# A recurrent attention followed by a token and channel mixer on one core: batch 0 in token slots on 64-row tiles, u of batches 1 to 3 transposed by DMA, another order

## The chip, the cores and the metric

The kernel runs on one core of one Trainium2 chip. The metric is the device time of one execution in microseconds (us). The engines are PE (TensorE, matrix products), DVE (VectorE), ACT (ScalarE), POOL (GpSimd) and SP, which here only issues transfers. Each engine works its own queue in order. An instruction whose operand isn't ready holds up everything behind it on that engine. ACT also issues some transfers.

## The reference

```python
# q, k, v, alpha: 4 batches x 8 heads x 768 tokens x 48, fp32
state = zeros(B, H, 48, 48)
for t in range(768):
    state = alpha[:, :, t, :, None] * state + k_t (outer) v_t
    y[:, :, t] = q_t @ state
x = y as (4, 768, 384)                       # heads side by side
xt = x.transpose(0, 2, 1)                    # batch, channel, token
h = max(xt @ w_tok1, 0) @ w_tok2             # 768 -> 256 -> 768 over tokens
u = x + h.transpose(0, 2, 1)
out = u + max(u @ w_ch1, 0) @ w_ch2          # 384 -> 1536 -> 384 over channels
```

## The kernel before

The recurrence is worked in chunks of 256 tokens: three chunks for each of 4 batches, n = 0 to 11, n = 3b + k. A chunk is loaded with two neighbouring tokens on each of the 128 partitions; the two are its slots. A half is 128 tokens: 64 partitions with both slots. In a chunk the decay is made explicit by cumulative sums of ln alpha: `E` is the exponential of the sum, `IE` that of its negative. q is scaled by E and k by IE (`scaled`, line 642). Then come

- the transposes of the scaled k and q (names `trk`, `trq`, matmuls on line 654, copied out of PSUM as `evk`, `evq`; from chunk 6 on transfers that transpose, `dk`, `dq`, line 664, with a copy `pq`),
- `G`, the products of keys and queries of a half (16 small matmuls, through `mm`, line 593), times a triangular mask (`mask`, line 700),
- `K`, the product of keys and values that goes into the state, and the state itself (`s`: first multiply, line 747; `sa`: add, line 750; `sm`: multiply by the decay, line 753),
- `ia`, `ib` (queries times the state) and `y` (masked G times v), summed in one PSUM bank, and its copy `x` (line 684 on ACT, 685 on DVE).

Batch 0 (`WIDE`, chunks 0 to 2) takes the cumulative sum for each token (768 columns, `cumw`). The other chunks multiply the two alphas of a partition first (`P`, line 578) and correct one slot (`k0a`, `q0r`, lines 634 and 638). For y and K the kernel wants the 128 tokens of a half on 128 partitions, while the loads have them as 64 partitions times two slots. So half of v (`vs0`, `vs1`) and of the scaled k (`ka`, `kb`, `kc`) is copied between partition halves, 64 rows by 384, by `copy` (lines 684, 685), on all twelve chunks.

The mixer of a batch: `t1` (w_tok1, line 787), `ht` (relu), `t2` (w_tok2, line 792), `u` (add of x, line 796), u transposed (`ut`), `c1` (w_ch1, line 811; 12 column blocks by two halves, three matmuls each), `rt` (relu, line 782 on ACT, 784 on DVE), `c2` (w_ch2, line 816; 6 row blocks by four groups of three matmuls), `o` (line 820), `st` (store). For batches 0 and 1 (`UP`) u is transposed by TensorE (`up`, line 803, 18 matmuls, and three copies); for 2 and 3 by two transfers each (`ux`, line 668).

Loads are fp32, 384 KB each: alpha, k, q and v of 12 chunks (line 534) and 16 pieces of the weights (lines 550 to 557), into 19 shared buffers (`in`). Weight pieces are cast to bf16 once (`cw`).

The order of the work isn't left to a scheduler. `build` declares the operations, and three tables say the rest: ORDER lists all operations in one sequence with a letter for the engine (t PE, v DVE, s ACT, g POOL, y SP), and so fixes each engine's queue; BUFS gives each operand its buffer; GATES is empty. Waits follow from data and from buffers used again. `shared` (called by `copy` and the two-operand operations on DVE and POOL) makes such an operation wait for the last one of the other of these two engines, since they share a port. So DVE and POOL take turns there, in ORDER's sequence.

ORDER of before also holds fillers (`f1_`, `f3_`: one or three matmuls of 128x128 by 512 columns on a tile of zeros, `fill`), whose results nobody reads: 38 matmuls, all ahead of the first `c1` of batch 0.

Of the kernel before, what the change touches and what calls it, by code (L numbers as in the profile page):

```python
# [97 lines left out]
NX = 6  # L98
KFN = 0
LAST = (3, 0)  # L100
UP = (0, 1)
# [9 lines left out]
WIDE = (0, 1, 2)  # L111

# [3 lines left out]
def build(g):  # L116
# [8 lines left out]
    def filler(nm, bank):  # L125
        return [P.op(f"f{z}_{nm}", {"PE": pe([512] * z)["PE"], "NONE": (0.0, 0.0)}, -100, writes=[bank],
                     emit=lambda e, z=z: g.fill(bank, z)) for z in (1, 3)]

    def attention(n):
# [5 lines left out]
        def O(name, eng, i, **kw):  # L135
            return P.op(f"{name}{n}", eng, pr(i), **kw)

        def fill(nm, bank):
            return filler(f"{nm}{n}", bank) if n < NB else []

        at, kt, qt, vt = V("in"), V("in"), V("in"), V("in")
        ld = {}
        for v, nm in ((at, "at"), (kt, "kt"), (qt, "qt"), (vt, "vt")):
            ld[nm] = P.op(f"ld_{nm}{n}", {"SP": (420.0, 420.0), "ACT": (374.0, 374.0)}, -90000.0 + 10 * n, writes=[v],
                          emit=lambda e, v=v, nm=nm: g.load(e, nm, v, b, k, ld[nm]), dma=("i", IN_NS, 1500.0, 650.0))
        la, E, IE = V("la"), V("E"), V("IE")
        pkk, pkq, vb = V("pkk"), V("pkq"), V("vb")
        k_in, q_in = [ld["kt"]], [ld["qt"]]
        if n in WIDE:
            lnp = O("ln", act(800, True), 0, writes=[la], reads=[at], preds=[ld["at"]], emit=lambda e: g.lnw(la, at))  # L150
            cb = V("pair")
            cum = O("cumw", pe([384] * 4 + [4] * 8 + [16]), 2, writes=[cb, E, IE], reads=[la], preds=[lnp] + fill("cumw", cb),
                    emit=lambda e: g.cumw(cb, la))
            e1 = O("E", act(768), 4, writes=[E], reads=[cb], preds=[cum], emit=lambda e: g.exps(E, cb, 1.0))
            et = O("Et", act(16), 6, writes=[E], reads=[cb], preds=[cum], emit=lambda e: g.exptot(E, cb))
            e2 = O("IE", act(768), 3, writes=[IE], reads=[cb], preds=[cum], emit=lambda e: g.exps(IE, cb, -1.0))
        else:
# [8 lines left out]
            e1 = et = O("E", act(400), 4, writes=[E], reads=[cb], preds=[cum], emit=lambda e: g.expE(E, cb))  # L166
            e2 = O("IE", act(384), 4, writes=[IE], reads=[cb], preds=[cum], emit=lambda e: g.expIE(IE, cb))
# [5 lines left out]
        kk = O("kk", either(dve(768), pool_tt(768)), 5, writes=[pkk], reads=[kt, IE], port=True, preds=k_in + [e2],  # L173
               emit=lambda e: g.scaled(e, pkk, kt, IE, wide))
        qq = O("qq", either(dve(768), pool_tt(768)), 5, writes=[pkq], reads=[qt, E], port=True, preds=q_in + [e1],
               emit=lambda e: g.scaled(e, pkq, qt, E, wide))
# [3 lines left out]
        if n < NX:  # L180
            bk, bq = V("one"), V("one")
            trk = O("trk", pe([128] * 8), 8, writes=[bk], reads=[pkk], preds=[kk] + fill("trk", bk),
                    emit=lambda e: g.trw(bk, pkk))
            evk = O("evk", either(dve(1024, True), act(1024)), 9, writes=[tpk], reads=[bk], preds=[trk],
                    emit=lambda e: g.trwev(e, tpk, bk))
            trq = O("trq", pe([128] * 8), 8, writes=[bq], reads=[pkq], preds=[qq] + fill("trq", bq),
                    emit=lambda e: g.trw(bq, pkq))
            evq = O("evq", either(dve(1024 * 1.065), act(1024 * 1.34)), 9, writes=[tpq], reads=[bq], preds=[trq],
                    emit=lambda e: g.qev(e, tpq, g.bank(bq).bitcast(BF16)))
        else:  # L190
            evk = O("dk", {"SP": (1240.0, 1240.0)}, 9, writes=[tpk], reads=[pkk], preds=[kk],
                    emit=lambda e: g.xbar(tpk, pkk), dma=("x", 1400.0, 1180.0, 480.0))
            tqx = V("tpk")
            xq = O("dq", {"SP": (1240.0, 1240.0)}, 9, writes=[tqx], reads=[pkq], preds=[qq],
                   emit=lambda e: g.xbar(tqx, pkq), dma=("x", 1400.0, 1180.0, 480.0))
            evq = O("pq", either(dve(1024), act(1024 * 1.35, True), {"POOL": (1100.0, 1140.0)}), 9.5, port=True, writes=[tpq], reads=[tqx], preds=[xq],
                    emit=lambda e: g.qev(e, tpq, g.t(tqx)))
        gtm = V("gtm")
        masks = []
        for hf in range(2):  # L200
            gp = V("pair")
            G = O(f"G{hf}_", pe([128] * 4), 10 + hf, writes=[gp], reads=[tpk, tpq], preds=[evk, evq] + fill(f"G{hf}", gp),
                  emit=lambda e, hf=hf, gp=gp: g.gmm(gp, tpk, tpq, hf), mode="G")
            masks.append(O(f"mask{hf}_", dve(1024), 12 + hf, writes=[gtm], reads=[gp], preds=[G],
                           emit=lambda e, hf=hf, gp=gp: g.mask(gtm, gp, hf)))
        nst = 2 if k < NB - 1 else 1
        kp = V("pair")
# [4 lines left out]
        vsw = lambda hf, preds: shift(f"vs{hf}_", 10, [vb], [vt], preds, lambda e: g.vswap(e, vb, vt, hf))  # L212
        turned = n >= KFN
        if turned:
            vs = [vsw(hf, [vc]) for hf in range(2)]
            kx, kp_in = None, [kk, vc, vs[0]]
            if nst == 2:
                kx = V("kt")
                ka = shift("ka", 9, [kx], [pkk], [kk], lambda e: g.kturn(e, kx, pkk, 0))
# [137 lines left out]
    for b in range(B):  # L357
        mixer(b)
# [516 lines left out]
```

## Time and profile before

| | us |
|---|---|
| median of 3 runs | 167.82 |
| lowest and highest | 167.51, 168.41 |
| the profiled execution, first to last instruction (span) | 165.0 |

| engine | busy us | share of the span |
|---|---|---|
| PE | 156.2 | 95% |
| DVE | 121.2 | 73% |
| ACT | 96.2 | 58% |
| POOL | 68.7 | 42% |

The profile is of one execution. Its slices divide the span into 40 equal parts of 4.125 us; a digit is the busy share in tenths. In a row of the chain stand the start, the length and the engine with the line; in a row of the groups the line, engine, operation, operands, count, then busy us, the mean ns of one, and the idle time before with what ended it. In a row of a stretch stand its bounds, its length, and busy us with the count of instructions for each engine. A timeline row has start, length, engine, line, operation, operands, count. "SPq" is the transfer queue of SP.

### The profile page before, as it was taken

The numbers are of one execution on the slowest core, as the hardware profiler recorded it, in microseconds if no ns is written. First come the engines' busy times: TensorE is split into PE (matmuls) and PEld (weight loads), VectorE is DVE, ScalarE is ACT, GpSimd is POOL, SyncE is SP. The second block draws the span as 40 slices with busy tenths as digits, with TensorE's granted clock in tenths as the row PEclk, the third lists the DMA queues.
The fourth block names the chain that finished last, engine by engine and source line by source line (L and its number), as shares of the span: only waits on it lengthen the run. The fifth ranks groups of instructions, "written<-read, shape, count | busy, mean of one in ns | idle before, by whom it ended". The sixth has DMA issues, their size and how long they took to land.

```text
span 165.0 us, 4235 instructions
## 1 busy us (share of the span) xinstructions
PE 156.2 (95%) x1683; PEld 99.2 (60%) x1683; DVE 121.2 (73%) x210; ACT 96.2 (58%) x186; POOL 68.7 (42%) x84
## 2 busy tenths in 40 slices
PE   7969769999999999999999999999999999999992
PEld 2435446666666766576666666666666656656662
DVE  4098989989898898798878999989492455524422
ACT  3599987998877837939887746913614001514110
POOL 4025659497217475792388528973300000000000
PEclk9999999999999999999999999999999999999999
DMA  4999999999999999999989996898001136200213
GB/s 121 324 325 325 337 347 316 365 327 352 371 335 347 326 315 226 307 252 264 136 198 255 211 250 120 219 181 183 0 4 48 49 75 157 105 0 0 99 72 119
DMA packets 74531, 34.48 MB, mean 209 GB/s; under 512 B 67984, under 2 KB 73488, under 8 KB 74512
## 3 DMA queue, kind: packets, MB, share of 16 engines
q1 hardware_dynamic: 50576, 23.30, 55.2%
q10 hardware_dynamic: 23936, 10.91, 24.3%
q8 instruction: 13, 0.21, 0.5%
q14 instruction: 6, 0.05, 0.1%
HBM read 25.17 MB, written 4.72 MB: 181 GB/s over the span
## 4 chain that ended last, share of the span: by engine, by line
PE 83%; DMA 4%; SPq 3%; POOL 2%; issue 2%; ACT 2%; DVE 1%; POOLq 0%; DVEq 0%
PE ps L816 29%; PE ps L811 29%; PE ps L593 14%; PE ps L792 5%; DMA in<-in_v_dram 4%; PE ps L787 4%; SPq L534 3%; PE ps L654 1%; PE ps L803 1%; POOL pkk L642 1%; DVE gtm L700 1%; POOL vb L685 1%; ACT x L684 1%; POOL ss L753 1%; ACT E L626 0%
## 5 line engine op out<-in xcount | busy, mean ns | idle before, releaser
L816 PE MATMUL ps<-wc,rt 128*128 128x384 bf16 (+1 forms) x300 | 54.7, 320 | 0.0
L811 PE MATMUL ps<-ut,wc 128*128 128x384 bf16 x288 | 51.3, 326 | 0.0
L782 ACT ACTIVATE rt<-ps 128x384 bf16<-128x384 f32 x54 | 24.4, 490 | 35.4 <-PE ps L811 34.7
L811 PEld LDWEIGHTS <-wc 128*128 128x128 bf16 x288 | 27.1, 98 | 16.7
L816 PEld LDWEIGHTS <-rt 128*128 128x128 bf16 x300 | 27.5, 98 | 15.9
L700 DVE TENSOR_TENSOR gtm<-ps,mk 128x1024 bf16<-128x1024 f32 x24 | 28.7, 1219 | 4.8 <-PE ps L593 3.4
L784 DVE TENSOR_SCALAR rt<-ps 128x384 bf16<-128x384 f32 x42 | 21.7, 551 | 9.2 <-PE ps L811 9.2
L820 DVE TENSOR_TENSOR o<-ps,u 128x384 f32<-128x384 f32 (+1 forms) x25 | 13.1, 537 | 10.0 <-PE ps L816 9.1
L685 POOL CAST vb<-in 64x384 bf16<-64x384 f32 (+1 forms) x18 | 10.9, 608 | 15.2 <-DVE pkk L642 8.9
L593 PE MATMUL ps<-zs 128*128 128x512 bf16 x38 | 12.7, 452 | 2.9 <-DVE zs L496 1.1
L684 ACT CAST x<-ps 128x384 bf16<-128x384 f32 x17 | 7.8, 477 | 10.7 <-PE ps L593 10.5
L796 DVE TENSOR_TENSOR u<-ps,x 128x384 bf16<-128x384 f32 x24 | 11.8, 550 | 3.0 <-PE ps L792 3.0
L642 DVE TENSOR_TENSOR pkq<-in,E 128x768 bf16<-128x768 f32 x8 | 7.6, 954 | 5.4 <-ACT E L626 5.2
L787 PE MATMUL ps<-x,wt 128*128 128x384 bf16 x48 | 11.1, 325 | 0.5 <-DVE gtm L700 0.4
L684 ACT CAST vb<-in 64x384 bf16<-64x384 f32 (+1 forms) x18 | 11.1, 618 | 0.7 <-DMA in<-in_v_dram 0.2
L642 POOL TENSOR_TENSOR pkk<-in,IE 128x768 bf16<-128x768 f32 x5 | 9.1, 1816 | 4.9 <-DVE pkk L685 3.2
L753 POOL TENSOR_TENSOR ss<-tmp,E 128x384 bf16<-128x384 f32 x11 | 9.2, 833 | 3.2 <-DVE tmp L750 2.9
L750 DVE TENSOR_TENSOR tmp<-ps,ss 128x384 f32<-128x384 f32 x16 | 8.8, 552 | 1.0 <-PE ps L593 0.5
L792 PE MATMUL ps<-ht,wt 128*128 128x384 bf16 x48 | 9.5, 326 | 0.0
L593 PEld LDWEIGHTS <-gtm 128*128 128x128 bf16 x192 | 7.4, 96 | 2.7 <-DVE gtm L700 0.9
L593 PEld LDWEIGHTS <-tpk 48*64 48x64 bf16 x384 | 6.1, 106 | 4.9 <-issue 4.3
L593 PE MATMUL ps<-vb,gtm 128*128 128x48 bf16 x192 | 8.6, 183 | 0.4 <-DVE gtm L700 0.4
(91 smaller groups left out, 216.6 us busy)
## 6 DMA issues: line engine op xcount, KB each, us to landing
in<-in_moe_w_ch_dram SPq DMA_DIRECT2D x10, 384.0 KB, 6.2
in<-in_alpha_dram SPq DMA_DIRECT2D x9, 384.0 KB, 6.8
out_dram<-o SPq DMA_DIRECT2D x16, 192.0 KB, 2.5
in<-in_q_dram SPq DMA_DIRECT2D x7, 384.0 KB, 6.3
in<-in_v_dram ACTq DMA_DIRECT2D x7, 384.0 KB, 6.0
in<-in_k_dram ACTq DMA_DIRECT2D x6, 384.0 KB, 5.7
in<-in_k_dram SPq DMA_DIRECT2D x6, 384.0 KB, 6.2
in<-in_v_dram SPq DMA_DIRECT2D x5, 384.0 KB, 7.2
```

The source lines that it names most:

```text
L593: return self.pe.matmul(out, lhsT=lhsT, rhs=rhs, start=start, stop=stop, skip_group_check=True)
L642: self.shared(self.eng[e].tensor_tensor(self.t(dst)[:, :, :, 0:D], self.t(src).rearrange("p h s d -> p s h d"), bass.AP(tensor=f.tensor, o ...
L684: return self.act.copy(d, s)
L685: return self.shared(self.eng[e].tensor_copy(d, s))
L700: self.nc.vector.tensor_tensor(self.t(gtm)[:, hf, :, :], self.pair(gp).rearrange("p a (j t) -> p (a j) t", t=128), bass.AP(tensor=m.tensor ...
L782: self.act.activation(d, s, AF.Relu)
L784: self.nc.vector.tensor_scalar_max(d, s, 0.0)
L787: self.pe.matmul(self.bank(bank)[:, 0:HD], lhsT=self.wt1[:, kc, m * 128 : m * 128 + 128], rhs=self.t(x), start=(kc == 0), stop=(kc == NS - 1))
L792: self.pe.matmul(self.bank(bank)[:, 0:HD], lhsT=self.wt2[:, kc, i * 128 : i * 128 + 128], rhs=self.t(hts[kc]), start=(kc == 0), stop=(kc = ...
L811: self.pe.matmul(self.bank(bank)[:, 0:HD], lhsT=self.wc1[:, kc, mc * 128 : mc * 128 + 128], rhs=self.t(ut)[:, 3 * half : 3 * half + 3, kc, ...
L816: self.pe.matmul(self.bank(bank)[:, 0 : cz - ca], lhsT=self.t(rts[mc][0])[:, i * 128 : i * 128 + 128], rhs=self.wc2[:, mc, ca:cz], start=( ...
L820: self.nc.vector.tensor_tensor(self.t(o)[:, ca:cz], self.bank(bank)[:, 0 : cz - ca], self.t(u)[:, i % 3, ca:cz], ALU.add)
```

## The change

1. **Batch 0 by slot.** In chunks 0 to 2 G isn't formed for a half but for the keys of one slot: 64 keys of each half against the 128 queries of their own half, in the two halves of the partitions (`gslot`). The mask is shifted by one column for one of the slots (`maskslot`, a new table `mkw`). y is then the sum over both slots, with 64-row products: 32 matmuls of 48 columns for a chunk (`yslot`), and K 16 matmuls of 96 columns for two halves (`khalf`; 8 in chunk 2, which needs one half). The copies `vs`, `ka`, `kb`, `kc` of these chunks go: 13 in all.
2. **State of batch 0.** The earlier state is added to K in PSUM by a matmul with the identity (`kadd`, named `A`, 384 columns, four of them); one multiply by the decay follows (`s`). The pairs `sa`, `sm` of batch 0 go (four). The small exponential `Et` goes into `E` (a group of 16 columns more in `cumw`).
3. **UP is (0,)**: u of batch 1 goes by two transfers as in batches 2 and 3; 18 matmuls and three copies go.
4. **Fillers** may stand ahead of any PE operation of batch 0 and 1 in the order; every three of a filler are one fp32 matmul, 64x64 by 384 columns, the rest as before. ORDER has 14 of the bf16 kind and 8 in fp32, all ahead of the first `c1`. The tile of zeros is now a piece of an `rt` buffer.
5. **w_ch1 pieces** 0 to 2 are cut by columns (256 columns of all 384 rows), so that a column block needs one piece; pieces 3 to 5 as before.
6. **Loads**: those of chunks 0 to 5 and of the weights go only by SP's queue, later ones by SP or ACT. Before, nine of these went by ACT (alpha 1, k 0, k 2, the first piece of w_tok1, q 5, v 4, v 5 and two pieces of w_ch2).
7. **ORDER and BUFS are new throughout.** What matters for the prediction:
   - SP's loads begin alpha 0, q 0, k 0, alpha 1, alpha 2, v 0, alpha 3, k 1, q 1, v 2, k 2, q 2, v 1, k 3, alpha 4, v 3, two pieces of w_tok1, q 3, two of w_tok2, k 4, and then the w_ch1 pieces 4, 3, 5 (23rd to 25th).
   - POOL takes the scalings of q 0, q 1, k 2, q 2, k 3, q 3; DVE those of k 0 and k 1. Before, DVE had seven of the first eight.
   - The first `c1` of batch 0 uses pieces 3, 4, 5 in both kernels.
   - Between the last t2 that a transfer of u needs and the first c1 that reads it stand fewer PE operations than before (batch 1: two c2 groups, a t2, a cumulative sum, seven c2 groups).
   - At the end the last PE work is again one half-width block of batch 3 (4 times 3 matmuls of 192 columns), its 96 KB store goes by SP, and a store of 192 KB by ACT beside it.

```diff
-NX = 6
+KX = (6, 7, 8, 9, 10, 11)
+QX = (6, 7, 8, 9, 10, 11)
...
-UP = (0, 1)
+UP = (0,)
...
+LOADQ = ({"SP": (420.0, 420.0)}, {"SP": (420.0, 420.0), "ACT": (400.0, 400.0)})
...
+        if wide:
+            kps = [V("one") for _ in range(nst)]
+            K = O("K", {"PE": (430.0, 560.0)}, 9.5, writes=kps, reads=[pkk, vb], preds=kk + [vc],
+                  emit=lambda e, first=before is None: g.khalf(kps, pkk, vb, first), mode="Y")
+            for hf in range(nst):
+                kp, s_, sp = kps[hf], V("ss"), states[-1]
+                KO = K
+                if sp is not None:
+                    KO = O(f"A{hf}_", pe([384]), 9.6 + hf, writes=[kp], reads=[sp[0]], preds=[K, sp[1]],
+                           emit=lambda e, kp=kp, s0=sp[0]: g.kadd(kp, s0))
+                so = O(f"s{hf}_", dve(384), 10 + hf, writes=[s_], reads=[kp, E], preds=[KO, et],
+                       emit=lambda e, s_=s_, kp=kp, hf=hf: g.sfirst(s_, kp, E, hf, wide))
+                states.append((s_, so))
...
     def fill(self, bank, count):
-        for _ in range(count):
-            z = self.zs
-            z = bass.AP(tensor=z.tensor, offset=z.offset, ap=[list(z.ap[0]), [0, 4], [1, 128]])
-            self.mm(self.bank(bank), self.zs, z, True, True)
+        z, w = self.zs, self.zs.bitcast(F32)
+        for _ in range(count // 3):
+            m = bass.AP(tensor=w.tensor, offset=w.offset, ap=[list(w.ap[0]), [0, 6], [1, 64]])
+            self.mm(self.bank(bank)[0:64, 0:384], w, m, True, True)
+        for _ in range(count % 3):
+            m = bass.AP(tensor=z.tensor, offset=z.offset, ap=[list(z.ap[0]), [0, 4], [1, 128]])
+            self.mm(self.bank(bank), z, m, True, True)
...
+    def gslot(self, gp, tpk, tpq, sl):
+        tk, tq = self.t(tpk), self.t(tpq)
+        for j in range(4):
+            for hf in range(2):
+                for r in range(2):
+                    pr = slice(r * 64, r * 64 + D)
+                    self.mm(self.bank(gp, r)[hf * 64 : hf * 64 + 64, j * 128 : j * 128 + 128],
+                            tk[pr, (sl * 4 + j) * 128 + hf * 64 : (sl * 4 + j) * 128 + hf * 64 + 64],
+                            tq[pr, j * 256 + hf * 128 : j * 256 + hf * 128 + 128], True, True)
...
+    def khalf(self, kps, pkk, vb, first):
+        kk, vv = self.t(pkk), self.t(vb)
+        for j in range(4):
+            for sl in range(2):
+                for hf, kp in enumerate(kps):
+                    ph = slice(hf * 64, hf * 64 + 64)
+                    self.mm(self.bank(kp)[:, 96 * j : 96 * j + 96], kk[ph, sl, 2 * j : 2 * j + 2, :],
+                            vv[ph, sl, 2 * j : 2 * j + 2, :], j == 0 and sl == 0, (first and hf == 0) and sl == 1)
+
+    def kadd(self, kp, s0):
+        self.mm(self.bank(kp)[:, 0:HD], self.idn, self.t(s0), False, True)
+
+    def yslot(self, yps, gtm, vb, first):
+        gg, vv = self.t(gtm), self.t(vb)
+        for h in range(H):
+            for sl in range(2):
+                for hf in range(2):
+                    ph = slice(hf * 64, hf * 64 + 64)
+                    self.mm(self.bank(yps[hf])[:, h * D : h * D + D], gg[ph, sl, 4 * (h % 2) + h // 2, :],
+                            vv[ph, sl, h, :], first[hf] and h == 0 and sl == 0, h == H - 1 and sl == 1)
```

409 lines of the change are left out of this document (222 added, 187 removed), and 22 rows, old and new, of the table BUFS.

## The prediction

> **What bounds the kernel now.** I read the page first: the busy shares, the 40 slices and the shares of the chain of waits.
>
> ```profile
> span 165.0 us, 4235 instructions
> PE 156.2 (95%) x1683; PEld 99.2 (60%) x1683; DVE 121.2 (73%) x210; ACT 96.2 (58%) x186; POOL 68.7 (42%) x84
> ...
> PE   7969769999999999999999999999999999999992
> ...
> DVE  4098989989898898798878999989492455524422
> ...
> GB/s 121 324 325 325 337 347 316 365 327 352 371 335 347 326 315 226 307 252 264 136 198 255 211 250 120 219 181 183 0 4 48 49 75 157 105 0 0 99 72 119
> ...
> PE 83%; DMA 4%; SPq 3%; POOL 2%; issue 2%; ACT 2%; DVE 1%; POOLq 0%; DVEq 0%
> ```
>
> TensorE is full from the eighth slice (29 us) to the end, and has holes only ahead of it. So there are two regimes. To separate them I took the busy time per stretch, cutting at the first w_ch1 product and at the last matmul, which I found in the chain told in order of time.
>
> ```profile
> 14.06 7.23 DMA in<-in_v_dram
> ...
> 37.51 2.48 PE ps L811 x15
> ...
> 49.12 0.17 PE ps L593 x4
> ...
> 50.27 0.45 PE ps L654 x8
> ...
> 53.12 0.27 PE ps L593 x6
> ...
> 71.03 0.67 PE ps L803 x12
> 71.70 0.49 PE ps L816 x3
> 72.19 0.34 PE ps L803 x6
> ...
> 161.97 0.03 issue
> ```
> ```profile
> core 0: us, PE busy (x) PEld busy (x) DVE busy (x) ACT busy (x) POOL busy (x), PEclk, DMA share, GB/s
> 4.10:8.50 4.40, 4.40 (x36) 2.26 (x35) 0.00 (x0) 2.40 (x4) 0.00 (x0) 1.00 1.17 325
> ...
> 8.50:36.40 27.90, 23.30 (x362) 15.31 (x360) 25.44 (x35) 25.44 (x45) 17.68 (x23) 1.00 1.11 334
> 37.50:162.00 124.50, 124.39 (x1255) 79.64 (x1252) 92.38 (x156) 65.97 (x136) 47.98 (x49) 1.00 0.73 180
> ```
>
> In the dense stretch (37.5 to 162.0) TensorE is busy 124.39 of 124.50 us: only fewer instructions shorten it. In the start (8.5 to 36.4) it is 23.30 of 27.90, and of that 6.8 us is filler, as the same stretch shows for the tile of zeros alone:
>
> ```profile
> 8.50:36.40 27.90, 6.80 (x23) 1.67 (x21) 0.00 (x0) 1.00 1.11 334
> ```
>
> There VectorE and ScalarE are each busy 25.44 of 27.90 us (91%), with DMA at 334 GB/s beside them. So the start is a tight row of small operations, above all on VectorE, that ends with the adds that form u of batch 0. After the last matmul stand 3.0 us of store, and the timed median (167.82 us) is 2.8 above the span; I carry both over.
>
> **Dense stretch, part by part.** The three transposing groups of batch 1's u (18 matmuls) go: 0.67 + 0.34 = 1.01 us by the two chain rows above. The new order puts one cumulative sum and one state product behind the first w_ch1 product that stood ahead of it (+0.27, +0.17), and one key transpose ahead (-0.45), the rows of 53.12, 49.12 and 50.27; these cancel. 124.46 us (161.97 - 37.51) becomes 123.45.
>
> In their place stand two DMA transposes of u, and batches 2 and 3 keep theirs, but all stand closer to their first use.
>
> ```profile
> tpk<-pkk SPq DMA_TRANSPOSE x6, 5.3
> ...
> ut<-u SPq DMA_TRANSPOSE x4, 3.2
> ```
> ```profile
> 32.90 2.15 PE L792 MATMUL ps<-ht,wt 128*128 128x384 bf16 x12
> ...
> 33.49 2.88 DVE L796 TENSOR_TENSOR u<-ps,x 128x384 bf16<-128x384 f32 x6 [0.33 <-PE ps L792]
> ```
> ```profile
> 102.79 1.48 DVE L796 TENSOR_TENSOR u<-ps,x 128x384 bf16<-128x384 f32 x3
> ```
> ```profile
> 104.30 1.31 SPq L668 DMA_TRANSPOSE ut<-u  x1
> ```
> ```profile
> DMA to landing us min/median/max: 3.2/3.2/3.9
> ```
>
> The last row belongs to the view of the tile that holds u transposed; in that with the queue's rows an issue occupies SP for 1.3. Three adds take 1.48 us: 0.47 apart, 0.55 for one. Batch 0's first add began at 33.49 (second row of the timeline above), 0.6 after its two matmuls did; 0.33 of that is the two, so 0.27 passes from matmul to add. Batch 1, first half: from its last t2 product to the first w_ch1 product the new order has two ch2 groups (0.49 each by the row of 71.70), a t2 (0.33), a cumulative sum (0.27) and seven ch2 groups (3.4), 5.0 us; the adds take 1.2; 3.8 is left for 3.2 to 3.9. Batch 2: 3.93 of work, 0.8 to the add, 3.1 left. Batch 3: 4.9, 1.3, 3.6 left. Waits in all: 0.1 us at 3.2 us each, 1.2 at 3.9; if batch 1's lands like the key transposes, which run beside loads (5.3), 1.5 more on its half. I take 0.4. The adds on VectorE and the SP issue (1.3 us each) have room: VectorE is busy 92 of 124 us. What is queued behind the SP issue is the stores and later transposes; none is due within 1.3 us.
>
> **The start, part by part.** Batch 0 loses 13 copies between partitions (6 of v, 7 of k), four pairs of state add and state multiply (each becomes one multiply after an identity matmul), and the separate small exponentials.
>
> ```profile
> L700 DVE TENSOR_TENSOR gtm<-ps,mk 128x1024 bf16<-128x1024 f32 x24 | 28.7, 1219 | 4.8 <-PE ps L593 3.4
> ...
> L642 DVE TENSOR_TENSOR pkq<-in,E 128x768 bf16<-128x768 f32 x8 | 7.6, 954 | 5.4 <-ACT E L626 5.2
> ...
> L642 POOL TENSOR_TENSOR pkk<-in,IE 128x768 bf16<-128x768 f32 x5 | 9.1, 1816 | 4.9 <-DVE pkk L685 3.2
> ```
> ```profile
> L684 ACT CAST vb<-in 128x768 bf16<-128x768 f32 x6 | 5.0, 835 | 0.3 <-DMA in<-in_v_dram 0.2
> ...
> L747 DVE TENSOR_TENSOR ss<-ps,E 128x384 bf16<-128x384 f32 x4 | 2.2, 548 | 0.0
> ...
> L685 DVE COPY tpk<-ps 128x1024 bf16<-128x1024 bf16 x4 | 2.6, 683 | 0.0
> ```
> ```profile
> 8.52 0.96 DVE L642 TENSOR_TENSOR pkq<-in,E 128x768 bf16<-128x768 f32 x1 [5.19 <-ACT E L626]
> ```
> ```profile
> 10.27 1.30 DVE L685 COPY tpq<-ps 128x1024 bf16<-128x1024 bf16 x1
> ```
> VectorE's queue ahead of and with the six adds of u, by these durations: before 28.5 us (7 scalings, 6 masks, 2 query and 3 key copies, 8 of the states, 10 others with the adds), laid end to end from 8.52 to 36.37 (the end of the six adds above). After: 24.0 (2 scalings instead of 7, since GpSimd takes them; the same masks; 7 of the states; x, cast and adds). The masks read another table of the same size and keep their 1.22. On GpSimd the chunk 0 to 3 scalings take 1.82 each, six of them 10.9 us.
>
> Where they stand in time is a walk down the queues by hand. A load is 393 kB, 1.21 us at 325 GB/s; the first slice's 121 GB/s puts the beginning of the flow at 2.6 us, so load n lands at 2.6 + 1.21n. (Check: the 15th by that at 20.8; the chain's load lands at 21.3.) All early loads now go down SP's queue, alpha of chunk 0 first: 3.9 us instead of 5.0. Then, start times: chunk 0's k scaling on VectorE 7.2; key copy 8.9; query copy 10.8 (behind GpSimd's scaling); mask 13.5 (behind the third cumulative sum); chunk 1's k scaling 15.45 (GpSimd's scaling before it waits for the ninth load, 13.5); mask 16.8; key copy 17.9; mask 19.5 (after its G); then nearly back to back mask, state, query copy, state, x, state, masks 24.9 and 26.0, four short ones, x of chunk 2 28.9, state add, ht 29.9, cast 30.3; t2 begins at 30.95, the adds run from 31.5 to 34.35; the last copy that the first w_ch1 product needs ends at 35.2. So 35.3, against 37.5. I left out some hand-offs and add 0.5: 35.8, a gain of 1.7.
>
> A floor: the 25th load is the last w_ch1 piece that this product needs, as it was before; 32.9 landed, 33.8 with its 0.83 cast (the ScalarE casts of this size take 0.835). More than 3.7 us can't come out of the start.
>
> New operations, bounded: the identity matmul (384 columns) is a c2 matmul's 0.16 us. K by halves is 16 matmuls of 96 columns where 8 took 0.35 (two fours, 0.18 from the one's start to the other's):
>
> ```profile
> 12.66 0.42 PE L593 MATMUL ps<-tpq,tpk 48*64 48x128 bf16 x16
> ...
> 14.56 0.34 PE L593 MATMUL ps<-vb,pkk 128*128 128x96 bf16 x4 [0.28 <-POOL pkk L685]
> 14.74 0.33 PE L593 MATMUL ps<-vb,kt 128*128 128x96 bf16 x4
> ```
>
> 0.35 if the halves overlap as in G (first row: 16 of 128 columns in 0.42), 0.7 if not. The y form has 32 of 48 columns, 0.45 or 0.8. I take the overlap (nearest row, G); without it 6 x 0.35 = 2.1 us of TensorE, of which perhaps half lies on the path: 1.0.
>
> Fillers: 38 become 14 of the same kind and 8 in fp32 with 384 columns on a quarter of the array.
>
> ```profile
> 1.05 5.73 PE L593 MATMUL ps<-zs 128*128 128x512 bf16 x15 [1.05 <-DVE zs L496]
> ```
> ```profile
> 13.01 0.82 PE L593 MATMUL ps<-zs 128*128 128x512 bf16 x3
> ```
>
> The first twelve stand 0.43 us apart, those after 5.7 us 0.22 (three in 0.82, the last drawn out to its end), though the granted clock reads 1.00: half rate until TensorE has worked some 4.6 us. An fp32 one isn't in the trace: at least one pass, 0.16; at most four at half rate, 1.28 each. I take 0.65, three of the present kind, between. Doubled, they cost 5 us in all, but only two, ahead of the third cumulative sum, stand before a path with no slack over 0.34: about +1.
>
> By the Trainium skill, FP8 and Floating Point Precision (Matmul Precision), a true fp32 matmul is four passes: 4 x 0.16 = 0.64, an estimate by that page, the sum unchanged. No row here shows it.
>
> **Sum.** 35.8 + 123.45 + 0.4 = 159.65 for the last matmul, 161.97 before: -2.3. The tail: the last add and its 96 kB store as before; a 192 kB store on the other queue starts 0.6 us earlier and lands 0.6 us later, so equal. Span 162.7, time 167.8 - 2.3 = 165.5.
>
> **Rivals.** (1) The start doesn't shorten: POOL's slow scalings and the single load queue stand in its in-order chain, first w_ch1 product at 37.5 again. For it: GpSimd's 1.8 us each and the shared-port waits; against: VectorE's 4.5 us less. Only the 1.01 stays, less 0.4: 167.2.
>
> (2) Transposes of u land late, between queued loads. For: 5.3 us for keys at 60 to 90 us; against: 3.9 at most for u so far. 1.5 on each of batch 1's halves and 1.2 elsewhere, less the 0.4 in the sum: 165.5 + 3.8 = 169.3 with the start as forecast; decides above 3.8 us landing.
>
> (3) Slower by the clock: the fillers don't hold the full rate. TensorE's start has 19 us of real work, some 12 of it ahead of t1. If that runs at half rate as the first twelve fillers did, it takes up to 12 us longer; about a third of it lies between VectorE operations on the path: +4, 169.5. It decides once t1, from 28.1 in the walk, begins after 30.4. For: eight fillers work on a quarter of the array; against: there is real work in every slice.
>
> The Trainium skill, TensorE: Matmul & The Clock Gate (What's actually happening), has the default throttled, and about 3.4 us of activity to lift it; the 4.6 us of the fillers row agree roughly. By that rule idle windows bring half rate back, which is (3).
>
> **How the numbers follow.** Forecast 0.50 (own range 164 to 167); rival 1 0.20; rival 2 0.13; rival 3 0.17. From no change the measurement can tell 0.5%, 0.84 us: faster is below 167.0, slower above 168.7. Faster: 0.50 of the forecast, 0.08 of the first rival and 0.04 of the second, 0.62; same 0.17; slower 0.21. The range reaches up to rivals 2 and 3 and down to most of the start's floor: 163.6 to 169.4.
>
> **What would show it.** The dense stretch from the first w_ch1 product to the last matmul should be 123.5 to 124.5 us, with no idle over 0.5 ahead of the first products of batches 1, 2, 3. That product should start at 35 to 36.5, t2 near 31 to 32, VectorE's first mask near 13.5. Half-rate matmuls after 8 us, fp32 fillers over 0.8 us, or an idle TensorE beside a landing transpose would make it wrong.

## The result, and the profile after

The changed kernel takes 169.51 us (median of 4; 168.80 to 170.40), the kernel before 167.66 (4; 167.39 to 168.41). The ratio is 1.0133, 95% interval 1.009 to 1.0176: slower by 1.3%. Timed again on two other chips it came to 167.89 (1.0063, 1.0032 to 1.0094) and 168.14 (1.0037, 1.001 to 1.0064), so the loss is real and between 0.1 and 1.8%, about 0.6% over these 24 executions. Forecast was 165.5. All ratios leave out executions more than 1.5% above the fastest of the same kernel (one or two in e1, e4, e8 and e9 below); the medians hold them.

The page of the changed kernel: span, TensorE's busy line, its 40 slices (4.18 us each), the shares of the chain of waits.

```profile
span 167.2 us, 4297 instructions
PE 157.2 (94%) x1732; PEld 98.5 (59%) x1732; DVE 115.4 (69%) x206; ACT 95.6 (57%) x178; POOL 68.8 (41%) x78
...
PE   7999988999999999969999979989999999999992
...
PE 33%; DMA 2%; DVE 1%; issue 0%; DVEq 0%
```

The holes of the start are nearly gone, and three have come into the stretch that had none: the 18th, 24th and 27th digit fall off, which begin at 71.1, 96.1 and 108.7 us. The chain, 83% TensorE before, is 33% now: followed back from the end it leaves TensorE at a transpose of batch 2's u, landed at 109.2 us, and ends a few operations of VectorE further back, at 102.9. The busy time by stretch, cut at the first w_ch1 product and the last matmul as the prediction cut it, and in pieces of it:

```profile
core 0: us, PE busy (x) PEld busy (x) DVE busy (x) ACT busy (x) POOL busy (x), PEclk, DMA share, GB/s
36.80:164.08 127.28, 123.60 (x1240) 78.93 (x1238) 89.44 (x149) 70.67 (x141) 46.03 (x48) 1.00 0.76 189
...
60.00:80.00 20.00, 18.39 (x141) 11.23 (x139) 13.54 (x28) 11.70 (x26) 10.93 (x11) 1.00 0.99 233
80.00:100.00 20.00, 18.78 (x268) 12.45 (x266) 15.77 (x24) 14.21 (x26) 12.14 (x12) 1.00 1.00 228
100.00:120.00 20.00, 19.16 (x177) 11.92 (x176) 16.83 (x30) 12.25 (x27) 8.39 (x10) 1.00 0.91 181
```

The dense stretch is 127.28 us where it was 124.46. Its work shrank by 0.79 (124.39 to 123.60), its idle time grew from 0.1 to 3.68 us. The start gained 0.7 (37.51 to 36.80). So -0.7 - 0.8 + 3.6 + 0.1 of tail gives the +2.2 of the span (165.0 to 167.2). (The 37.51 is the chain's; in the timeline of the kernel before that product begins at 37.34, overlapping the matmul ahead of it, and by that the start gained 0.5 and the work shrank by 1.0.) What the idle time waited for, in the view of TensorE's waits (total, times, longest) and in its timeline (the bracket is the idle time before, with what ended it):

```profile
PE ps L894 <- DMA ut<-u: 2.5, 2, 1.6
PE ps L870 <- ACT E L680: 1.2, 1, 1.2
```
```profile
72.22 0.65 PE L894 MATMUL ps<-ut,wc 128*128 128x384 bf16 x3
74.48 1.80 PE L894 MATMUL ps<-ut,wc 128*128 128x384 bf16 x10 [1.61 <-DMA ut<-u]
...
98.47 0.32 PE L870 MATMUL ps<-x,wt 128*128 128x384 bf16 x1 [1.22 <-ACT E L680]
...
109.24 0.99 PE L894 MATMUL ps<-ut,wc 128*128 128x384 bf16 x5 [0.84 <-DMA ut<-u]
```

**The first wait (1.61).** It is for `ux_1_1`, the transpose of the second half of batch 1's u. The first half, `ux_1_0`, is issued at 66.76 and read at 70.47 without a wait. VectorE's timeline and the rows of SP's queue ahead of it:

```profile
65.67 1.49 DVE L879 TENSOR_TENSOR u<-ps,x 128x384 bf16<-128x384 f32 x3 [0.77 <-PE ps L875]
67.08 0.95 DVE L704 TENSOR_TENSOR pkk<-in,IE 128x768 bf16<-128x768 f32 x1
68.06 0.26 DVE L747 COPY kt<-pkk 64x384 bf16<-64x384 bf16 x1
68.88 0.35 DVE L747 CAST vb<-in 64x384 bf16<-64x384 f32 x1 [0.56 <-ACT vb L746]
69.26 0.56 DVE L879 TENSOR_TENSOR u<-ps,x 128x384 bf16<-128x384 f32 x1
```
```profile
66.76 1.33 SPq L730 DMA_TRANSPOSE ut<-u  x1
68.14 1.05 SPq L628 DMA_DIRECT2D out_dram<-o  x2
69.85 1.28 SPq L730 DMA_TRANSPOSE ut<-u  x1
```

The addend of the last add (`u_1_3`) was ready at 66.8, the end of its t2 product, but ORDER has three operations of chunk 6 ahead of it on VectorE, one of which stands 0.56 for ScalarE. It ends at 69.8. On SP's queue two stores stand ahead of the transpose; they are issued by 69.2, so here the add is the later of the two. The transpose is issued at 69.85 and lands 4.6 us later; TensorE wanted it at 72.87, 6.1 us after the t2 product.

**The second (1.22).** ScalarE's timeline (ACTq is a transfer that it issues):

```profile
94.01 0.37 ACTq L582 DMA_DIRECT2D in<-in_q_dram  x1
94.27 0.53 ACT L638 ACTIVATE la<-in 128x384 bf16<-128x384 f32 x1
94.50 0.52 ACTq L582 DMA_DIRECT2D in<-in_k_dram  x1
94.69 0.51 ACT L638 ACTIVATE la<-in 128x384 bf16<-128x384 f32 x1
95.05 2.44 ACTq L628 DMA_DIRECT2D out_dram<-o  x1
97.53 0.49 ACT L683 ACTIVATE IE<-ps 128x384 f32<-128x384 f32 x1 [2.33 <-issue]
97.92 0.50 ACT L680 ACTIVATE E<-ps 128x400 f32<-128x400 f32 x1
```

Issuing the store `st_0_0` keeps ScalarE for 2.44 us, where the two loads just ahead took 0.37 and 0.52. The exponentials `IE9` and `E9` stand behind it. E9 frees the PSUM bank that the t1 product at 98.47 needs; that is the second wait.

**The third (0.84).** E9 also feeds GpSimd's scaling of q, and VectorE stands for that, with batch 2's u behind. VectorE's, TensorE's and SP's timelines:

```profile
100.40 0.56 DVE L696 TENSOR_TENSOR in<-in,in 128x384 f32<-128x384 f32 x1 [2.00 <-POOL pkq L704]
...
103.70 2.87 DVE L879 TENSOR_TENSOR u<-ps,x 128x384 bf16<-128x384 f32 x6
```
```profile
103.68 0.81 PE L875 MATMUL ps<-ht,wt 128*128 128x384 bf16 x4
```
```profile
105.21 1.27 SPq L730 DMA_TRANSPOSE ut<-u  x1
```

The transpose of the half that is read first needs the third of these adds. It is issued at 105.21 and lands 3.99 us later, 0.84 after TensorE wanted it (108.40). But VectorE's standing hardly reaches it: TensorE is late with the t2 products too, and from the end of the last one that the half needs (104.33) to the issue pass 0.88 us; in e3 below, where ScalarE isn't held up, it is 0.78. What is long here is the landing.

### The profile page after: what moved, and what is told of

It reads as the page before. It is cut to its first block, busy times and chain, and to the rows that moved or that the text cites. A ratio compares the mean times of both kernels' runs of the same rounds, so it can differ in the third digit from the quotient of the medians.

```text
span 167.2 us, 4297 instructions
## 1 busy us (share of the span) xinstructions
PE 157.2 (94%) x1732; PEld 98.5 (59%) x1732; DVE 115.4 (69%) x206; ACT 95.6 (57%) x178; POOL 68.8 (41%) x78
## 5 line engine op out<-in xcount | busy, mean ns | idle before, releaser
L865 ACT ACTIVATE rt<-ps 128x384 bf16<-128x384 f32 x61 | 28.1, 492 | 26.8 <-PE ps L894 26.4
L867 DVE TENSOR_SCALAR rt<-ps 128x384 bf16<-128x384 f32 x35 | 18.2, 553 | 13.7 <-PE ps L894 13.6
L762 DVE TENSOR_TENSOR gtm<-ps,mk 128x1024 bf16<-128x1024 f32 x18 | 21.4, 1219 | 1.9 <-PE ps L647 1.7
L704 POOL TENSOR_TENSOR pkq<-in,E 128x768 bf16<-128x768 f32 x9 | 16.3, 1814 | 9.9 <-DVE pkk L704 5.4
L879 DVE TENSOR_TENSOR u<-ps,x 128x384 bf16<-128x384 f32 x24 | 11.8, 551 | 6.9 <-PE ps L875 6.9
L647 PE MATMUL ps<-rt 128*64 128x384 f32 (+1 forms) x30 | 12.3, 510 | 1.1 <-DVE rt L539 1.1
L746 ACT CAST vb<-in 64x384 bf16<-64x384 f32 (+1 forms) x18 | 11.8, 657 | 1.2 <-PE ps L647 0.9
L747 POOL CAST vb<-in 64x384 bf16<-64x384 f32 (+1 forms) x10 | 6.3, 632 | 9.1 <-DVE wc L747 3.0
L632 POOL TENSOR_TENSOR in<-in 128x384 f32<-128x384 f32 x7 | 7.0, 1001 | 6.4 <-DVE in L632 4.3
L778 DVE TENSOR_TENSOR gtm<-ps,mkw 128x1024 bf16<-128x1024 f32 x6 | 7.2, 1220 | 2.6 <-PE ps L647 2.6
L647 PE MATMUL ps<-tpq,tpk 48*64 48x128 bf16 x384 | 8.4, 220 | 0.2
L647 PE MATMUL ps<-vb,gtm 128*128 128x48 bf16 (+1 forms) x240 | 8.4, 182 | 0.1
```

The source lines that it names most:

```text
L647: return self.pe.matmul(out, lhsT=lhsT, rhs=rhs, start=start, stop=stop, skip_group_check=True)
L704: self.shared(self.eng[e].tensor_tensor(self.t(dst)[:, :, h0:h1, 0:D], self.t(src)[:, h0:h1].rearrange("p h s d -> p s h d"), bass.AP(tens ...
L746: return self.act.copy(d, s)
L762: self.nc.vector.tensor_tensor(self.t(gtm)[:, hf, :, :], self.pair(gp).rearrange("p a (j t) -> p (a j) t", t=128), bass.AP(tensor=m.tensor ...
L865: self.act.activation(d, s, AF.Relu)
L867: self.nc.vector.tensor_scalar_max(d, s, 0.0)
```

## The experiments

In this table the idle time is that of TensorE from the first w_ch1 product to the last matmul, the length of that stretch less its busy time, in the profiled execution. The ratio is to the kernel before on the same chip.

| kernel | first w_ch1 product | idle after it | span | median us (executions) | ratio, 95% interval |
|---|---|---|---|---|---|
| before | 37.51 | 0.1 | 165.0 | 167.66 (4) | 1 |
| changed | 36.80 | 3.7 | 167.2 | 169.51 (4) | 1.0133, 1.009 to 1.0176 |
| e5, e13: changed, again | 35.96, 37.66 | 3.1, 2.9 | 165.8, 167.3 | 167.89 (10), 168.14 (10) | 1.0063, 1.0037 |
| e1: `st_0_0` by SP | 35.97 | 1.8 | 164.4 | 166.61 (10) | 0.9959, 0.9925 to 0.9993 |
| e2: u_1_3, ux_1_1 first | 36.23 | 2.1 | 164.8 | 166.28 (10) | 0.9952, 0.9929 to 0.9976 |
| e3, e12: both | 37.03, 36.30 | 0.6, 0.9 | 164.0, 163.5 | 165.47 (4), 165.37 (6) | 0.9896, 0.9906 |
| e4: u of batch 1 by TensorE | 36.65 | 3.2 | 167.6 | 168.39 (10) | 1.0079, 1.0041 to 1.0118 |
| e6: u_1_3 first, on VectorE only | 36.80 | 1.2 | 164.5 | 166.74 (10) | 0.9996, 0.9966 to 1.0026 |
| e7: store ahead of the loads | 36.04 | 2.1 | 164.7 | 166.55 (10) | 0.9968, 0.9946 to 0.9991 |
| e8: both, v of chunk 3 early | 36.58 | | | 165.94 (12) | 0.9945, 0.9921 to 0.9968 |
| e9: bf16 fillers | 35.92 | 3.1 | 166.1 | 167.64 (10) | 1.0024, 0.9985 to 1.0062 |
| e10: no fillers | 40.16 | 0.5 | 167.2 | 169.13 (4) | 1.0118, 1.0077 to 1.0158 |
| e11: both, four o | 36.55 | 1.3 | 164.5 | 165.26 (6) | 0.9894, 0.9859 to 0.993 |
| e14: both, u of batch 1 by TensorE | 36.13 | 2.3 | 166.0 | 167.71 (10) | 1.0031, 0.9996 to 1.0066 |
| e15: q load of chunk 10 by SP | 37.02 | 3.9 | 167.8 | 169.56 (4) | 1.0114, 1.007 to 1.0158 |

**e1, e2, e3: two edits, one at a time and together.** Letters in ORDER: v VectorE, s ScalarE, y SP.

```diff
# e1
-... G1_8t st_0_0s st_1_2y ...
+... G1_8t st_0_0y st_1_2y ...
# e2
-... u_1_5v ln18s ux_1_0y ... kk6v kb6v ... st_0_5y ... vs0_6v st_0_3y u_1_3v ... c1_1_8_0t ux_1_1y ...
+... u_1_5v u_1_3v ln18s ux_1_0y ux_1_1y ... kk6v kb6v ... st_0_5y ... vs0_6v st_0_3y ... c1_1_8_0t ...
# e3: both
```

> The changed kernel with one store of batch 0 (st_0_0) issued by SyncE instead of ScalarE, at the same place in the order. Theory (the loss is three waits in the dense stretch, two of which go back to ScalarE being held up for 2.44 us at 95.05 issuing this store): the waits of 1.22 us before 98.47 and of 0.84 us before 109.24 go, the one of 1.61 us before 74.48 stays; 167.4 to 167.8, that is 1.7 to 2.1 below the changed kernel. Rival (the dense stretch is bound by what the other engines supply, so a wait taken away comes back at the next eviction): within 0.5 of the changed kernel, 169 to 170, with PE waits of 3 us or more still in the dense stretch.

> The changed kernel with the addition of u_1_3 moved ahead of the two casts of k and the shift copy that stood before it on VectorE, and its transpose ux_1_1 moved ahead of the two stores on SyncE's queue. Theory (u_1_1's transpose is late by its place in two queues, not by its landing time): the transpose is issued at 67 to 68 instead of 69.85 and lands by 72, the wait of 1.61 us before 74.48 goes, the other two stay; 167.7 to 168.1. Rival (supply-bound stretch): the casts and the copy that are moved back are late instead, an idle time of 1 us or more shows at the next eviction; 169 to 170.

> Both edits, the store on SyncE and u_1_3 with its transpose first. Theory: all three waits go, PE idle in the dense stretch falls from 3.7 us to under 0.5; 165.7 to 166.3, below the kernel before by 1.4 to 2. Rival: 168.5 or more, with idle time of PE moved to other places.

With the store on SP's queue, IE9 begins at 94.16, right behind the second load's issue (93.31, 0.80 long), and the wait for E is gone; 1.2 us for `ux_1_1` stays, as expected. So do 0.6 of the 0.84 for batch 2's transpose, which the expectation put down to the store: that was wrong. With u_1_3 first, both transposes of batch 1 are issued back to back, and `ux_1_1`, now ahead of the stores, lands after 2.9 us:

```profile
66.18 2.74 SPq L730 DMA_TRANSPOSE ut<-u  x2
68.97 1.05 SPq L628 DMA_DIRECT2D out_dram<-o  x2
```

No wait for a transpose of u is left, batch 2's among them (it lands after 2.8 us), which was not expected; 1.4 for E stays, as expected, and 0.7 is new, where an add of o holds up a w_ch1 product. Both edits together leave 0.6 us, and 0.9 when run again:

```profile
36.30:160.44 124.14, 123.26 (x1240) 78.89 (x1238) 89.37 (x149) 70.76 (x141) 46.15 (x49) 1.00 0.75 192
```

That is the stretch of e12: 124.14 us long with 123.26 of work, the forecast's 123.45 + 0.4 nearly. The time, 165.4, is 1.0% below the kernel before. The rival, that a wait taken away comes back elsewhere, is false for this pair of edits. That batch 2's wait goes too is not explained by either edit (see e4 and e14). The single edits came out 0.8 and 1.4 us below the theory's ranges, which were laid against 169.5, while the changed kernel's usual time is nearer 168; e2 also took away batch 2's wait.

**e5 and e13: the changed kernel again.**

> The changed kernel itself, timed in as many rounds as the edits. Theory: 168.6 to 169.6 with the three waits of PE in their places (3 to 4 us in all). Rival (the profiled execution of it was an odd one): below 168, with one of the three waits gone.

> The changed kernel unedited, on the chip of the two other runs. Theory: slower than the kernel before by 0.3 to 1.3 per cent, 167.5 to 169.5, with PE waits of 3 to 4 us in the dense stretch. Rival (no loss, the earlier ones were of their chips): within 0.3 per cent.

The three waits stand in their places (DMA ut 2.3 and 2.0 us, E 0.9 and 1.0); what differs between the executions is above all the start, 35.96 to 37.66. The median of e5 lies below its range, that of e13 in it.

**e6 and e7: which queue holds what.**

```diff
# e6
-... u_1_5v ln18s ux_1_0y ... st_0_3y u_1_3v ... ux_1_1y ...
+... u_1_5v u_1_3v ln18s ux_1_0y ... st_0_3y ... ux_1_1y ...
# e7
-... ld_qt10s ... ld_kt10s G0_8t G1_8t st_0_0s ...
+... st_0_0s ld_qt10s ... ld_kt10s G0_8t G1_8t ...
```

> The changed kernel with u_1_3 moved ahead on VectorE as before, but ux_1_1 left behind the two stores on SyncE's queue. Theory (both queues hold it: VectorE until 69.8, SyncE's stores until about 69.2): the transpose is issued about 0.6 us earlier, the wait of 1.61 shrinks to about 1.0 us, the two others stay; 168.5 to 169. Rival (VectorE's queue alone held it): the wait goes as in the run that moved both; 166.3 or so. Rival (SyncE's queue alone): no change from the changed kernel, 169 to 169.6.

> The changed kernel with the store st_0_0 kept on ScalarE's queue, but ahead of the two loads ld_qt10 and ld_kt10 instead of behind them. Theory (ScalarE is held up by the third transfer issued within some 1 us on its queue, whichever it is): the store is issued in 0.4 to 0.6 us, the third issue, ld_kt10, takes 2 us or more, and the exponentials behind it are as late as before; 168.6 to 169.6. Rival (it is the store that takes so long to issue from ScalarE): the store still takes 2.4 us, now before the loads.

In e6 the transpose is issued at 69.29 instead of 69.85 and the wait for it is 0.8: VectorE's and SP's queue each hold a share, as the theory had it, though the time fell by more than its 0.6: batch 2's wait went too (its transpose landed after 2.9 us), and that for E fell to 0.4 (the store's issue took 1.62). In e7 the store's issue is short, as the theory had it, but the rest of it and the rival fail. ScalarE's timeline there:

```profile
92.99 0.36 ACTq L628 DMA_DIRECT2D out_dram<-o  x1
93.25 0.53 ACT L638 ACTIVATE la<-in 128x384 bf16<-128x384 f32 x1
93.38 0.46 ACTq L582 DMA_DIRECT2D in<-in_q_dram  x1
93.94 0.52 ACT L638 ACTIVATE la<-in 128x384 bf16<-128x384 f32 x1 [0.16 <-issue]
93.96 0.81 ACTq L582 DMA_DIRECT2D in<-in_k_dram  x1
94.81 0.49 ACT L683 ACTIVATE IE<-ps 128x384 f32<-128x384 f32 x1 [0.35 <-issue]
```

The store takes 0.36 when it is first, and the load that is now third 0.81, not 2; no wait for E is left. So it is neither the store as such nor the third place as such: it is long for a store behind two loads that are still under way. (A wait of 0.8 stays ahead of batch 2's first w_ch1 product. Its row names a mask, but in e3 the same product begins before that mask ends; the transpose landed at 106.72, just ahead of the product's start at 106.79.) The same three transfers in another order are worth about 1% (0.9968 against 1.0063 on one chip).

**e15: one load fewer ahead of the store.**

```diff
-... c2_1_1_1t ld_qt10s sa0_8v P11g lnP11s ld_kt10s ...
+... c2_1_1_1t sa0_8v P11g lnP11s ld_qt10y ld_kt10s ...
```

> The changed kernel with the load of q of chunk 10 issued by SyncE, so that on ScalarE's queue the store st_0_0 is the second of two transfers, not the third of three. Theory (ScalarE is held up by what is still under way on its queue): the store's issue falls from 2.1 to 2.4 us to 0.3 to 1, the wait before the third exponential shrinks below 0.5, 166.5 to 167.3. Rival (the store's issue is long because of what is under way on SyncE's queue or in all): it still takes 1.6 us or more; 167.5 to 169.

The mechanism came out (the store's issue takes 0.98, and no wait for E is left), the time did not: 169.56. The load of q for chunk 10 now stands ahead of that of k for chunk 9 on SP's queue, which is issued at 94.31 instead of 92.81. Its 6.5 to 7.4 us of landing end about when VectorE can scale, and u of batch 2 is late again, in VectorE's and TensorE's timelines:

```profile
100.91 0.56 DVE L696 TENSOR_TENSOR in<-in,in 128x384 f32<-128x384 f32 x1 [2.14 <-issue]
```
```profile
104.35 0.48 PE L875 MATMUL ps<-ht,wt 128*128 128x384 bf16 x2 [1.18 <-DVE o L903]
```

That this load was what VectorE stood for is read from its times; the row names only "issue". TensorE also waits 1.8 for `ux_1_1` and 1.0 for batch 2's transpose, which this edit didn't touch.

**e4 and e14: the DMA transposes themselves.** u of batch 1 by TensorE again, with the store on ScalarE (e4) and on SP (e14). In both u_1_3 stands as early as in e2.

```diff
-UP = (0,)
+UP = (0, 1)
...
-... ux_1_0y ... ux_1_1y ...
+... c2_0_1_1t up_1_0t ... ut_1_0s ... c2_0_1_2t up_1_2t ... ut_1_2v ... c2_0_1_3t up_1_1t ... ut_1_1v ...
```

> The changed kernel with u of batch 1 transposed by TensorE again (as in the kernel before), batches 2 and 3 by DMA. Theory: the wait of 1.61 us goes and 6 more groups of matmuls come back (0.33 us for each transpose unit, about 0.35 us of work in all for one batch: a third of the 1.01 that 18 matmuls took), the two other waits stay; 168.1 to 168.8. Rival (DMA transposes as such slow the stretch, by the traffic that they put on the DMA engines): the landing times of the other batches shorten too and the waits before 98.47 and 109.24 shrink; 167 or less. Rival (supply-bound): 169 to 170.

> Both edits of the dense stretch (store on SyncE, u_1_3 early) and u of batch 1 transposed by TensorE as in the kernel before: 18 matmuls and three copies come back. Theory (with the waits gone the DMA transposes are worth the matmuls that they replace): TensorE's busy time in the dense stretch goes from 123.3 to 124.3 or 124.8, time up by 1.0 to 1.5 on the 165.4 of both edits, 166.4 to 166.9. Rival (the DMA transposes cost as much in traffic and queue places): 165.2 to 165.7.

TensorE's work in the dense stretch rises to 124.77 and 124.61, 1.2 and 1.35 above the same orders with transfers (123.60 and 123.26): the prediction's 1.01 for 18 matmuls is about right, and e4's expectation, a third of it, was wrong; that its range held the time is luck. But in both a wait of 1.4 us for batch 2's transpose stands, though in e14 both edits are in, and e14's time, 167.71, is above its range. The view of the tile that holds u transposed, from 100 to 112 us, in e14:

```profile
DMA to landing us min/median/max: 4.0/4.4/4.7
```

and in e3 and e12, where the same transfers are issued 0.6 and 1.0 us earlier:

```profile
DMA to landing us min/median/max: 2.9/3.5/4.1
```

The prediction's 3.1 us of cover there is exact (issued at 102.90 in e3, wanted at 106.02): at 2.9 it is enough, at 4.7 it isn't. The same holds in every profiled execution of this kernel and its edits. For the transpose of batch 2's u that is read first, in us:

| | issue to where TensorE wants it | landing | wait |
|---|---|---|---|
| e2, e3, e12, e6 | 3.0 to 3.1 | 2.8 to 2.9 | none |
| e10, e11 | 3.2, 3.3 | 3.6, 3.7 | 0.5, 0.45 |
| e1 | 3.3 | 3.8 | 0.6 |
| changed, e5, e13 | 3.2 | 4.0, 3.9, 3.9 | 0.84, 0.74, 0.71 |
| e7, e15 | 3.3, 3.2 | 4.0, 4.1 | 0.8, 1.0 |
| e4, e14 | 3.2, 3.3 | 4.6, 4.7 | 1.4 |
| e9 | 3.2 | 5.2 | 2.1 |

The cover is the same whether ScalarE was held up or not; the landing alone makes the wait. What makes the landing long or short is not shown: the DMA engines' share from 100 to 120 us is 0.91 in the changed kernel and 0.94 in e3, and where u_1_3 stands early it is 2.8 to 2.9 in e2, e3, e12 and e6, but 3.7 in e11 and 4.6 and 4.7 in e4 and e14.

So e14 bounds the worth of batch 1's DMA transposes from above only: 2.1 us by the two ratios (1.0031 and 0.9906), 1.35 of it work.

**e8, e9, e10, e11: the start, the fillers, what is left.** e8 has both edits and loads v of chunk 3 before alpha of chunk 4, whose work is moved back. e9 has three bf16 matmuls of 512 columns in place of each fp32 one, 38 fillers in all as in the kernel before; e10 has none. e11 has both edits, with four buffers of o (18 of rt).

```diff
# e8
-... ld_at4y ... ld_vt3y ... P4g ... lnP4s ... ln14s cum4t ... IE4s ...
+... ld_vt3y ld_at4y ... vs0_3g P4g ... E3s lnP4s ln14s ... t1_0_1_4t cum4t ... cw_wt20s IE4s ...
# e9: fill() as in the kernel before
# e10: f1_, f4_, f6_, f8_ operations out of ORDER
# e11
-"rt": 20, "o": 3
+"rt": 18, "o": 4
```

> Both edits of the dense stretch, and in the start the load of v for chunk 3 issued ahead of that of alpha for chunk 4, with the work on chunk 4's alpha (product, logarithms, its prefix matmuls and the exponential IE4) moved behind the copies of chunk 3. Theory (the first product with w_ch1 varies from 36.0 to 37.0 with the landing of chunk 3's v, which the cast on ScalarE waits for): the cast starts by 24.5 and the first product at 35.7 to 36.2; 164.3 to 165.0. Rival (the start is bound by the bytes in flight, so the later loads move back instead): first product at 36.5 or later, 165.3 to 166.

> The changed kernel with its unread matmuls in bf16 as in the kernel before (one of 128x512 for each, none in fp32). Theory (the unread matmuls stand beside work that is late for other reasons): first product with w_ch1 at 36 to 37, three waits as in the changed kernel; within 0.5 of the changed kernel, 167.5 to 168.4. Rival (the fp32 matmuls block TensorE in the start): first product 0.5 to 1 earlier than 36.0, time below 167.3. Rival (they keep the clock up better): first product after 37.5, time above 168.8.

> The changed kernel without any unread matmul (their results are read by nothing, so the output stays). Theory: the matmuls of the start run at half their rate for longer than the 4.6 us seen with them (16 of 128x128 in 1.2 us instead of 0.6), which shows where the start waits for TensorE: first product 37.5 to 39, time 169 to 171. Rival (the start is set by loads and copies alone): within 0.5 of the changed kernel.

> Both edits of the dense stretch and a fourth buffer for o (two of the 20 buffers of rt are given up for it, their work keeping its order). Theory (what is left in the dense stretch, 0.6 us, is an addition of o on VectorE that stood for a store to leave its buffer): no wait of PE over 0.3 us in the dense stretch, 164.6 to 165.2. Rival (the store is late for everything behind it, or rt's fewer buffers hold the evictions): 165.3 to 166, with another wait in its place.

The first w_ch1 product follows ScalarE's cast of chunk 3's v by 11.3 to 11.8 us wherever the order of the start is the same. Its rows in e1 and in e3:

```profile
24.41 0.83 ACT L746 CAST vb<-in 128x768 bf16<-128x768 f32 x1
```
```profile
25.75 0.83 ACT L746 CAST vb<-in 128x768 bf16<-128x768 f32 x1 [1.44 <-DMA in<-in_v_dram]
```

In e1 the product starts at 35.97, in e3 at 37.03. In e8 the load comes early and the cast begins at 24.23, and yet the product starts at 36.58. Now the casts of two weight pieces wait instead (that execution took 168.27 us against a median of 165.94, so only its start is read here):

```profile
25.83 0.83 ACT L746 CAST wt<-in 128x768 bf16<-128x768 f32 x1 [0.76 <-DMA in<-in_moe_w_tok_dram]
26.89 0.83 ACT L746 CAST wt<-in 128x768 bf16<-128x768 f32 x1 [0.23 <-DMA in<-in_moe_w_tok_dram]
```

That is what the rival said, the later loads move back, and its range holds the time (165.94); one start is little to show it with. The kind of filler makes no difference that e9 shows. Without fillers the first w_ch1 product comes 3.4 us later than in the changed kernel's profile. TensorE's timeline in e10 and below it in the changed kernel, the first cumulative sum and some identity matmuls:

```profile
5.20 1.12 PE L646 MATMUL ps<-la,u 128*128 128x384 bf16 x3 [5.20 <-ACT la L640]
...
24.66 0.50 PE L646 MATMUL ps<-ss,idn 128*128 128x384 bf16 x1
...
27.20 0.33 PE L646 MATMUL ps<-ss,idn 128*128 128x384 bf16 x1
```
```profile
5.22 0.65 PE L647 MATMUL ps<-la,u 128*128 128x384 bf16 x3 [0.20 <-ACT la L641]
...
24.55 0.32 PE L647 MATMUL ps<-ss,idn 128*128 128x384 bf16 x1
```

Without fillers the same matmul takes 0.50 at 24.66 and 0.33 from 27.2 on: the start runs at the lower rate to about 27 us. But of the 3.4 us only 1 to 1.5 reach the end (169.13 against 167.64 in e9 on the same chip), because the waits of the dense stretch shrink to 0.5. With the same queue places as in the changed kernel, `ux_1_1` is issued at 73.21, lands after 2.8 us and is read at 76.08 without a wait, and the store `st_0_0` takes 1.14. A fourth o is worth nothing that can be told (0.9894 against 0.9906); its profiled execution shows other waits, 0.8 for a copy of GpSimd and 0.4 for a transpose.

## Why the prediction was wrong, point by point

**The step that failed** is "Waits in all: 0.1 us at 3.2 us each, 1.2 at 3.9 ... I take 0.4", with the sentences "The adds on VectorE and the SP issue (1.3 us each) have room" and "none is due within 1.3 us". It measured 3.7 us (3.1 and 2.9 in the repeats). Three things were wrong in it.

- *Cover without queues (1.61).* It counted how much TensorE has to do between the last t2 product and the first w_ch1 product, and took from it two hand-offs and the landing. For batch 1 it did so for the first half only, and there it was right. The second half, where the wait came, would have passed the same count: 6.1 us from the t2 product to where it is read, less 0.8 to the end of the add, is 5.3 for a landing of 4.6. That VectorE has room on the average says nothing of what stands ahead of `u_1_3` in its order: 2.2 us of chunk 6, and beside that 1.05 of stores on SP. e2 and e6 show it: the same work in other places, and the wait is gone or halved.
- *A landing time from another execution (0.84).* 3.2 to 3.9 us were the landings in the kernel before. The cover of 3.1 for batch 2 was right, but its transpose landed after 4.0, and `ux_1_1` after 4.6; over all executions the landings are 2.8 to 5.2. The text named longer ones (key transposes: 5.3) and gave them to rival 2; the sum took 0.4, between its own 0.1 and 1.2. In e10, with the same places, a short landing leaves no wait for `ux_1_1`: both the place and the landing are needed for the 1.61.
- *ScalarE's own transfers (1.22).* The prediction went through SP's queue and not through the transfers that ScalarE issues. A store behind two loads held ScalarE 2.44 us, and with it TensorE 1.22. e1 and e7 take this wait away in two ways.

**The dense stretch's work** was right: 123.45 predicted, 123.60 in the changed kernel, 123.26 in e12. With most of the waits gone, e3 and e12 take 165.4, the forecast nearly, but partly by luck: their spans, 164.0 and 163.5, are 1.3 and 0.8 above the forecast's 162.7, and the 1.1 us too much between span and time (below) makes up for it.

**The start** was mis-sized: 35.8 predicted, 36.80 measured, 35.96 to 37.66 over the executions with this order. The walk's early points hold (first mask 13.96 against 13.5; the 0.5 is alpha's first landing, 4.32 against 3.9), then it takes the load of v for chunk 3 as landed, and the cast of it waits up to 1.44 us. In e13, the latest, it is a load of v further ahead (cast at 21.79, 0.87 of wait). t2 begins at 32.47, not 30.95. The gain of 1.7 was 0.7, and is 0 to 1.5 as these loads happen to land.

**The new operations** cost what was taken: K by halves 16 in 0.51 at full rate (overlapped), the y form 32 in 0.57 (0.80 at 18.48), an fp32 filler about 0.70 against 0.65, with no effect on the time that e9 shows. By the Trainium skill, FP8 and Floating Point Precision (Matmul Precision), four passes would be 0.64; the trace agrees roughly.

**Time against span.** The sum added 2.8 us to a span. In each later profiled execution whose own time is shown it is 1.7 (168.9 - 167.2 here), so the profiled execution of the kernel before was one of its faster ones, 1.1 us under its median. In spans the miss is 4.5 us (162.7 to 167.2): 3.3 of waits, 1.0 of start, 0.15 of work.

**The rivals.** Rival 1 (the start doesn't shorten) is false on the whole, though one execution (37.66) is like it. Rival 2 (transposes of u late) named the right mechanism for two of the three waits, landings above 3.8 us (4.6 and 4.0), but its price came out by luck: of its 4.2 us for transposes 2.45 came, part of that by queue places (e2, e6), and 1.22 came from ScalarE, which it didn't have. Rival 3 (the clock) is false: the first cumulative sum runs at the full rate at 5.2 us (three in 0.65), and t1 begins at 27.55. e10 shows what it would have been: t1 at 31.37 and +3.4 on the start, near its +4.

## What to carry to other kernels

A cover is not the work between producer and reader on the busy engine: walk each queue that the operand passes (the adding engine, the issuing queue, the transfer), for every half that is read, and set down what stands ahead in it. Where the cover is as short as a landing time, price the wait at the longest landing seen, not the shortest: here the same transfer took 2.8 to 5.2 us. A transfer issued by an engine that also computes has a price at that place, by what is still under way on its queue; its order among its neighbours can be worth 1%. Where an order is new throughout, look for the two or three places where it has no slack, and move only those: here another queue for one store, and an earlier place for one add and its transpose, turned a loss into a gain of 1%.

## What the runs showed of the hardware

The issue of the same store from ScalarE took 0.36 us with nothing just ahead of it (e7), 0.98 behind one load (e15), and 1.14 to 2.59 behind two (1.14 in e10, 1.62 in e6, 2.44 here, 2.59 in e2), and ScalarE computed nothing for most of it (2.33 of the 2.44). The Trainium skill, Perfetto Trace Analysis (DMA Instruction — HWDGE), has the profiled length of such an instruction begin once its semaphores are satisfied, and hold the wait for the descriptor generator and the generating, with a buffer that can fill up. The rows agree so far that the length follows what is under way; SP's queue has no row from 93.3 to 100.3 us in the changed kernel, so no issue of SP stood beside it, and no run here tells what made it long.

A transpose of u (128 partitions, three blocks of 384) kept SP 1.24 to 1.57 us, at times 2.0 to 2.3, and landed after 2.8 to 5.2, at different places of the order and in different executions. And the changed kernel's start scatters by 1.7 us between executions of the same order, with the landing of its loads of v.
